# Elementwise work of GpSimd moved to VectorE in an attention, MLP and mixture-of-experts kernel

## Chip, core and metric

The kernel runs on one core of a Trainium2 chip. The metric is device time in microseconds (us), median of several executions; lower is better. Times of single instructions come from one execution taken with the hardware profiler.

## What is computed

Linear attention, a dense MLP and a top-1 mixture of experts run one after the other, all in float32 (4608 tokens, 512 features; the MLP has 2048 hidden features, each of 8 experts 1024):

```python
kv  = einsum('bhsd,bhse->bhde', k, v);  o = einsum('bhsd,bhde->bhse', q, kv)
x   = o / sqrt(mean(o*o) + 1e-6) * g_norm                     # as 4608 x 512
h   = x @ w_in;  x = (h * clip(h + 3, 0, 6) / 6) @ w_out      # float64 weights
do  = x @ w_skip > 0;  e = argmax(x[do] @ w_gate);  p = softmax(...)[e]
out = x;  out[do] += p * (relu(x[do] @ w1[e]) @ w2[e])
```

## The kernel before

**Three products for one.** A float32 product is made of three products of a faster format. Each operand is split into a high part (a copy by ScalarE, rounded) and a low part (operand minus high part, a two-input subtraction from SBUF). The products are high x high, high x low and low x high. So every weight, query, token column and gate value costs one ScalarE copy and one subtraction.

**The dense part.** Attention works on 16 units of 288 tokens, each in 4 pairs of heads; the MLP on 18 chunks of 256 tokens, each in 16 steps `f` of 128 hidden features. A step is `G1` (12 matmuls of 256 columns into `h`, L665), the gate `G1e`, and `G2` (6 matmuls of 512 columns into `y`, L656). The gate is four operations in a row: ScalarE `relu` (L701), VectorE `mul` (L706), ScalarE `high` (L710), and `low` (L716). The first two chunks run side by side while the MLP's weights are still being made.

**The weights of the MLP** are float64 and arrive as raw bits in 32 pieces: 16 for `w_in`, 16 for `w_out`, alternately. `convert` makes one piece in seven steps: `c1` to `c4` on VectorE (L600, L604, L607, L611), `c5` (L615), `high` on ScalarE (L618), `low` (L621). Four pieces can be under way: there are four staging slots in `SG` (a slot is loaded anew once `c5` has read it), and four buffers of the pool `row`.

**The routing.** After a chunk, nine scalar products on each of its two token tiles (`dot`, L768), the choice of an expert, a slot number, and a scatter of (token, gate) into a table by an indirect DMA of GpSimd (L857).

**The order.** Nothing is issued in the order of the Python text while the plan is open: `Plan.order` is a list scheduler. Each operation has an engine, a nominal cost, the operations it depends on, tokens of buffers, and a priority: the longest way from it to the end, plus a bias of its kind from the table `BIAS`. Whenever an engine is free in this calculation, the ready operation with the highest priority is taken. The outcome is a fixed order on each engine; on the chip each engine runs its own list strictly in order. Operations marked `"VP"` may go to VectorE or to GpSimd, whichever is free first, at 2.05 times the cost on GpSimd. Marked so are the low parts of queries (`ql`, L344), squares (`A2l`, L405), token columns (`Xl`, L515, and L460), the gate (`g`, step 4, L716), the last conversion pass `c5` (L615), the low parts of the MLP's weights (L621) and of the first experts' weights (`wlo`, L565).

**The experts.** Eight experts follow, by slots of up to 512 tokens in straight program order. While one computes, the weights of the next are split, 16 pieces an expert, by `w_split`: ScalarE makes the high part, and the low part goes to GpSimd for every third piece (`sp`: `n % 16 % 3 == 2`; two of 16 with at most 128 tokens), to VectorE for the others (L565). GpSimd also gathers the token rows (L900) and scatters the results (L932) by indirect DMA.

Of the kernel before, what the change touches and what calls it, by code (L numbers as in the profile page):

```python
# [16 lines left out]
NE, EFF = 8, 1024  # L17
# [34 lines left out]
class Plan:  # L52
    """Emission order of the dense part: a list schedule of operations on the engines.

    An operation has a name, an engine ("PE", "A", "V", "P", "S" for DMA queues, "VP" for either
    of two, "-" for none), a nominal cost, the names it depends on, and tokens of buffers that it
    takes and gives back. Those on the longest way to the end go first, but for a bias of their kind."""
# [31 lines left out]
    def order(self):  # L89
# [24 lines left out]
        wait = {e: [] for e in self.ENGINES}  # operations whose predecessors have started  # L114
        giving, t, dma_free, n_left = [], 0.0, 0.0, len(ops)

        def add_wait(i):
            eng = ops[i][1]
            for e in ("V", "P") if eng == "VP" else (eng,):
                r = 0.0  # L120
                for j in preds[i]:
                    fin, ej = done[j]
                    r = max(r, fin + (0.0 if e == "-" or ej == e == "PE" else self.SAME if ej == e else self.LAT))
                wait[e].append((-prio[i], i, r))
# [4 lines left out]
        while n_left:  # L129
            keep, nxt = [], []  # L130
            for g in giving:
                if g[0] <= t + 1e-9:
                    self.free[g[1]] += 1
                else:
                    keep.append(g)
                    nxt.append(g[0])
            giving = keep
            for e in self.ENGINES:
                if busy[e] > t + 1e-9:
                    nxt.append(busy[e])  # L140
                    continue
                best = None
                for w in wait[e]:
                    if w[1] in start:
                        continue
                    if w[2] > t + 1e-9:
                        nxt.append(w[2])
                    elif best is None or w < best:
                        take = ops[w[1]][5]
                        if all(self.free[k] >= take.count(k) for k in take):  # L150
                            best = w
                if best is None:
                    continue
                i = best[1]
                _, eng, cost, _, _, take, give, dma, _ = ops[i]
                wait[e] = [w for w in wait[e] if w[1] not in start and w[1] != i]
                for k in take:
                    self.free[k] -= 1
                start[i] = t
                fin = busy[e] = t + (cost * 2.05 if eng == "VP" and e == "P" else cost)  # L160
                if e == "S":
                    dma_free = max(fin + self.DMA_ISSUE, dma_free) + dma
                    fin = dma_free + self.DMA_LAT
                else:
                    fin += dma
                done[i] = (fin, e)
                giving += [(fin + self.LAT * (e != "-"), k) for k in give]
                nxt += [busy[e], fin, t + 1e-6 if e == "-" else fin]
                n_left -= 1
                for j in succs[i]:  # L170
                    left[j] -= 1
                    if not left[j]:
                        add_wait(j)
                        nxt.append(t + 1e-6)
            if n_left:
                nxt = [x for x in nxt if x > t + 1e-9]
                assert nxt, [o[0] for i, o in enumerate(ops) if i not in start and not left[i]]
                t = min(nxt)
# [5 lines left out]
def fused_kernel(ctx, tc, qT, kvm, kvr, gv, w_in, w_out, w9, w9t, w1, w2, cst, tokid, out):  # L184
# [24 lines left out]
    def op(name, eng, cost, fn, deps=(), take=(), give=(), dma=0.0, bonus=0.0):  # L209
        """into the plan, while there is one; emitted at once afterwards"""  # L210
        if plan[0] is not None:
            plan[0].add(name, eng, cost, fn, deps, take, give, dma, bonus)
        else:
            fn("V" if eng == "VP" else eng)

    # ---- constants: cst = [blockones 128 | identity 128 | triu 128 | iota 8 | ebase 8]
# [14 lines left out]
    # weights: 8 slots of 4 x 128 rows x 512, high and low parts; the last four hold attention  # L231
    # operands first
# [15 lines left out]
    # token columns: 3 slots of 4 x 128 features x 256 tokens, high and low parts  # L248
# [11 lines left out]
    # ================= attention =================  # L260
# [29 lines left out]
    # units 0 and 1 run before the tensor engine is busy: plain float32 products  # L290
# [44 lines left out]
    def st_q(u, p):  # L335
# [12 lines left out]
        op(("ql", u, p), "VP", 0.37, low, [("qh", u, p)], give=["q"] if u >= 3 else [])  # L348
# [8 lines left out]
    def prev(name, u, p):  # L357
        """from unit 2 on, pairs pass a stage in their order"""
        return [(name, u, p - 1) if p else (name, u - 1, 3)] if (u, p) > (2, 0) else []

    # accumulators: units 0 and 1 have banks that the dense MLP does not use yet
# [28 lines left out]
    def st_A2(u, p):  # L390
# [19 lines left out]
        if u >= 3:  # L410
            op(("A2h", u, p), "A", 0.33, high, [("A2", u, p)], take=["ss", "ss"])
            op(("A2l", u, p), "VP", 0.37, low, [("A2h", u, p)], give=["a"])
# [37 lines left out]
    def st_late():  # L450
        # chunk 3's first columns, kept until chunk 0 has left its buffer
# [11 lines left out]
        op("late l", "VP", 0.5, low, ["late h"], give=["row"])  # L463

    def st_N(u, p):
        # one Newton step on r = rsqrt(m / D + eps): r (3 - (m / D + eps) r^2) / 2
# [26 lines left out]
    def st_X(u, p):  # L493
# [7 lines left out]
        for c, off, done, n in parts:  # L501
# [21 lines left out]
            else:  # L523
                op(("Xh", u, p, c), "A", ca, high, [("N2", u, p)] + [("G1", c - 3, 15)] * (c >= 3))
                op(("Xl", u, p, c), "VP", cv, low, [("Xh", u, p, c)])
# [3 lines left out]
    # ================= weights =================  # L529
# [16 lines left out]
    # float32 weights of the experts, half a slot at a time through three buffers  # L546
# [20 lines left out]
    def w_split(g, j, pool=False):  # L567
        w_high(g, j)
        w_low(g, j, "P" if pool else "V")
        if j == 1:  # L570
            w_load(g + 3)

    # float64 weights arrive as raw bits: (low word, high word) of each element
# [3 lines left out]
    def convert(n, key, i):  # L577
        """float64 piece n to high and low parts.
        float32 bits = sign and top exponent bit | the rest of the exponent, mantissa"""
# [29 lines left out]
        def c4(_):  # L609
            # float32(low word) * 2^-52 * 2^exponent, added to the high word's value  # L610
# [31 lines left out]
        op(N("sg"), "VP", 0.6, c5, [N(4)])  # L642
        op(N("h"), "A", 0.52, high, [N("sg")] + war)
        op(N("l"), "VP", 0.6, low, [N("h")], give=["row"])
        op(("w", key, i), "-", 0.0, lambda _: None, [N("l")], bonus=SLACK.get("w", 0))

    # ================= dense MLP =================
    g_t, y_t = {}, {}

    def mm3(prods, first=True, last=True):  # L650
        """prods: (psum, (stationary high, low), (moving high, low)); the low moving or
        stationary part that is made last comes last"""
# [40 lines left out]
    def G1e(c, f):  # L693
# [29 lines left out]
        op(("g", c, f, 4), "VP", 0.34, low, [("g", c, f, 3)], give=[tk])  # L723
# [36 lines left out]
    # ================= routing =================  # L760
# [47 lines left out]
    def route(i):  # L808
        """routing of token tile i as operations"""
# [53 lines left out]
    def rt_bump():  # L863
        # expert 0's next free slot is at least 256 from here on
# [15 lines left out]
    # ================= experts =================  # L880
    # sets of (token columns high and low, token rows, table entries)
# [3 lines left out]
    def scatter_free(group, inst):  # L885
        """rows of one scatter are never those of another"""
# [5 lines left out]
    def ix_load(ix, row0, nt):  # L892
        """table entries of nt * 128 slots from row0 (an expression)"""
        nc.sync.dma_start(ix[:, 0:nt, :], tab[bass.ds(row0, nt * 128), :].rearrange("(t p) c -> p t c", p=128))

    def f_load(st, nt, ntok=NTOK):
        """token rows; a slot without a token keeps the row it had"""
# [40 lines left out]
    def VN(e, st, nt, side=(), late=False):  # L938
        """nt * 128 tokens, nt from 2 to 4;
        late: the side work of a step comes after its second product"""  # L940
# [27 lines left out]
        def g2(f):  # L968
# [7 lines left out]
            else:  # L976
                # tile by tile, so that the first ones leave early
# [18 lines left out]
    def V128(e, st, side=(), first=()):  # L996
        """up to 128 tokens"""
# [5 lines left out]
        def g1(hf, half):  # L1003
# [6 lines left out]
            if half == 1:  # L1010
                h = st[2][1 + hf]  # not in use with one tile of tokens
# [31 lines left out]
    # ================= emission =================  # L1043
# [14 lines left out]
    # ---- attention, and the dense MLP: chunks 0 and 1 side by side while the weights arrive  # L1058
# [58 lines left out]
    # the first experts' weights take the places of the dense ones  # L1117
# [11 lines left out]
    for g in range(11):  # L1129
# [3 lines left out]
        if g < 8:  # L1133
            for i in range(2):
                user = ("G1" if n % 2 == 0 else "G2", C, 3 + 4 * (n // 2))
                op(("wh", g, i), "A", 0.52, lambda _, g=g, i=i: w_high(g, i), [("wl", g), user])
                op(("wlo", g, i), "VP", 0.6, lambda e, g=g, i=i: w_low(g, i, e), [("wh", g, i)], bonus=10)
# [5 lines left out]
    # ---- block (0, 0), with the routing of the last chunk beside it  # L1143
    la, lb = 2 * NCH - 2, 2 * NCH - 1

    def sp(n0, n1):
        """splits of pieces, 16 to an expert"""
        return [lambda n=n: w_split(n // 2, n % 2, n % 16 % 3 == 2) for n in range(n0, min(n1, 16 * NE))]
# [20 lines left out]
    # ---- the rest of expert 0, then the other experts  # L1169
    for k in range(NE):  # L1170
# [18 lines left out]
        def tail():  # L1189
            """slots from 512 on"""  # L1190
# [26 lines left out]
        with c1.Else():  # L1217
            with tc.If(n_k > off + 128) as c2:
                VN(k, cur, 2, side(10, (5, 6, 7, 8), 2))
            with c2.Else():  # L1220
                sd = [[] for _ in range(11)]
                for q, (m0, m1) in V128_SPLITS.items():
                    m0, m1 = (max(n1 - 16 + m, n0) for m in (m0, m1))
                    sd[q] += [lambda n=n: w_split(n // 2, n % 2, n % 16 in (9, 13)) for n in range(m0, min(m1, 16 * NE))]
# [42 lines left out]
```

## Time and profile before

| | |
|---|---|
| median of 3 runs | 1375.92 us (1373.79 to 1377.61) |
| span of the profiled execution | 1371.7 us, 4.2 us less than the median |
| TensorE busy | 1254.1 us (91%), 7449 matmuls |
| VectorE busy | 895.2 us (65%), 2412 instructions |
| ScalarE busy | 600.7 us (44%), 1520 instructions |
| GpSimd busy | 405.5 us (30%), 424 instructions |

The span runs from the first to the last instruction. Busy is the time in which an engine had an instruction under way; a matmul's end is modelled, so a TensorE that is busy all the time need not run at its peak. The shares are averages over stages that differ a lot; the stages are seen in the rows below.

### The profile page before, as it was taken

Reading aid. Unit: us, or ns where it says so; the run is one execution under the profiler, and the core shown is the slowest. Engines: PE = TensorE matmul, PEld = TensorE weight load, DVE = VectorE, ACT = ScalarE, POOL = GpSimd, SP = SyncE. Lnnn points to the kernel's source line nnn. Section 1 sums busy time; section 2 is a strip of 40 time slices with the busy share of each in tenths; the row PEclk is TensorE's granted clock in tenths of the full one; section 3 lists DMA queues with packets and bytes.
Section 4 is the critical chain, followed back from the end, with each engine's and each line's share of the span. In section 5 each row is a group of like instructions: output and inputs, shape, how many; then the busy total and the mean of one; then the engine's idle time right before and its main releaser. Section 6 shows DMA issues by size and latency. Waiting matters only on the chain.

```text
span 1371.7 us, 21419 instructions
## 1 busy us (share of the span) xinstructions
PE 1254.1 (91%) x7449; PEld 1111.5 (81%) x7449; DVE 895.2 (65%) x2412; ACT 600.7 (44%) x1520; POOL 405.5 (30%) x424
## 2 busy tenths in 40 slices
PE   5788799999999999999999999999989867789895
PEld 4666688898889899999989999999878757768774
DVE  4999989748875757866767767775744344444531
ACT  2543364536563336545546546533533344324320
POOL 2656644314421103212212212200432333321411
PEclk9799999999999999999999999999999989999998
DMA  9333352211121111211121111001442355443500
GB/s 289 99 106 118 97 176 66 75 36 48 49 67 35 49 36 36 74 58 35 59 74 43 51 58 48 6 32 62 138 144 83 107 160 160 133 128 96 165 23 32
DMA packets 77449, 114.94 MB, mean 84 GB/s; under 512 B 16934, under 2 KB 38326, under 8 KB 77136
## 3 DMA queue, kind: packets, MB, share of 16 engines
q1 hardware_dynamic: 71184, 98.12, 23.0%
q0 software_dynamic: 6080, 14.57, 3.3%
q8 instruction: 89, 1.46, 0.5%
q14 instruction: 96, 0.79, 0.2%
HBM read 90.19 MB, written 25.79 MB: 85 GB/s over the span
## 4 chain that ended last, share of the span: by engine, by line
PE 68%; DVE 16%; issue 8%; DMA 4%; ACT 2%; POOL 1%; another core or an unknown queue 1%; SPq 0%; DVEq 0%; POOLq 0%; ACTq 0%
PE h L665 33%; PE y L656 29%; DVE junk L768 3%; DMA rows<-y_scr,idx 3%; PE kvp L300 2%; DVE wbits L604 2%; DVE SG L611 2%; DVE SG L607 2%; DVE t L706 1%; DVE wbits L600 1%; PE xp L912 1%; DMA sh<-cst 0%; DMA q<-qT 0%; PE h L656 0%
## 5 line engine op out<-in xcount | busy, mean ns | idle before, releaser
L768 DVE CUSTOM_DVE_ANT_0 junk<-ysb,w9b 128x512 bf16<-128x512 f32 x306 | 226.0, 739 | 4.9 <-ACT ysb L747 2.3
L701 ACT ACTIVATE t<-h,half 128x256 f32<-128x256 f32 x288 | 135.9, 473 | 205.8 <-PE h L665 104.1
L716 POOL TENSOR_TENSOR gl<-t,gh 128x256 fp32r<-128x256 f32 x120 | 103.3, 862 | 318.2 <-ACT gh L710 212.2
L710 ACT ACTIVATE gh<-t 128x256 fp32r<-128x256 f32 x288 | 119.5, 415 | 156.1 <-DVE t L706 104.6
L706 DVE SCALAR_TENSOR_TENSOR t<-t,h 128x256 f32<-128x256 f32 x288 | 119.5, 416 | 73.6 <-ACT t L701 71.7
L965 DVE SCALAR_TENSOR_TENSOR gl<-h,gh 128x256 fp32r<-128x256 f32 x64 | 27.1, 423 | 150.9 <-ACT gh L964 150.8
L716 DVE TENSOR_TENSOR gl<-t,gh 128x256 fp32r<-128x256 f32 x168 | 81.1, 483 | 63.4 <-PE y L656 31.9
L656 PE MATMUL y<-WH,gh 128*128 128x512 f32 x360 | 117.8, 405 | 0.0
L656 PE MATMUL y<-WH,gl 128*128 128x512 f32 x360 | 113.0, 391 | 3.6 <-DVE gl L716 3.6
L656 PE MATMUL y<-wh,gh 128*128 128x512 f32 x352 | 114.5, 404 | 1.2 <-ACT gh L710 1.1
L656 PE MATMUL y<-WL,gh 128*128 128x512 f32 x360 | 113.4, 392 | 0.0
L656 PE MATMUL y<-wl,gh 128*128 128x512 f32 x352 | 110.8, 394 | 1.7 <-DVE wl L621 1.7
L656 PE MATMUL y<-wh,gl 128*128 128x512 f32 x352 | 110.0, 391 | 0.1
L665 PE MATMUL h<-x12h,WH 128*128 128x256 f32 (+1 forms) x480 | 85.1, 301 | 24.7 <-issue 17.6
L964 ACT ACTIVATE gh<-h 128x256 fp32r<-128x256 f32 x64 | 24.5, 383 | 187.9 <-PE h L665 187.8
L665 PEld LDWEIGHTS h<-x12h,WH 128*128 128x128 f32 x480 | 75.7, 197 | 36.2 <-issue 18.6
L665 PE MATMUL h<-x12h,WL 128*128 128x256 f32 (+1 forms) x480 | 83.4, 297 | 0.0
L656 PEld LDWEIGHTS y<-WH,gl 128*128 128x128 f32 x360 | 67.4, 188 | 19.6 <-DVE gl L716 4.4
L665 PE MATMUL h<-x12l,WH 128*128 128x256 f32 (+1 forms) x480 | 82.5, 295 | 0.0
L656 PEld LDWEIGHTS y<-wl,gh 128*128 128x128 f32 x352 | 66.3, 189 | 18.1 <-DVE wl L621 2.6
L656 PEld LDWEIGHTS y<-WL,gh 128*128 128x128 f32 x360 | 67.8, 188 | 15.7
L656 PEld LDWEIGHTS y<-wh,gl 128*128 128x128 f32 x352 | 66.0, 188 | 15.6 <-DVE gl L716 0.6
(216 smaller groups left out, 2855.8 us busy)
## 6 DMA issues: line engine op xcount, KB each, us to landing
kv<-kvm SPq DMA_DIRECT2D x24, 512.0 KB, 4.1
stgh<-w SPq DMA_DIRECT2D x22, 512.0 KB, 3.7
stgl<-w SPq DMA_DIRECT2D x21, 512.0 KB, 4.0
stg<-w SPq DMA_DIRECT2D x21, 512.0 KB, 4.0
y_scr<-ysb SPq DMA_DIRECT2D x36, 256.0 KB, 2.5
final<-ysb SPq DMA_DIRECT2D x36, 256.0 KB, 2.7
SG<-w_in SPq DMA_DIRECT2D x16, 512.0 KB, 3.7
SG<-w_out SPq DMA_DIRECT2D x16, 512.0 KB, 3.5
```

The costliest lines, as they stand in the source:

```text
L300: nc.tensor.matmul(ps, t[0:n, 0, i, :], t[0:n, 1, i, :], start=(i == 0), stop=(i == 4))
L604: nc.vector.scalar_tensor_tensor(t, H, -(1 << 30), t, op0=ALU.bitwise_and, op1=ALU.bitwise_or)
L607: nc.vector.tensor_scalar(H, conv[n], -(1 << 23), None, op0=ALU.bitwise_and)
L611: nc.vector.scalar_tensor_tensor(f32(L), L.bitcast(U32), 2.0 ** -52, f32(H), op0=ALU.mult, op1=ALU.mult)
L656: nc.tensor.matmul(ps, st[a], mv[b], start=first and (a, b) == (0, 0) and all(p[0] is not ps for p in prods[:q]), stop=last and (a, b) == ...
L665: nc.tensor.matmul(ps, st[a], mv[b], start=first and (a, b) == (0, 0) and all(p[0] is not ps for p in prods[:q]), stop=last and (a, b) == ...
L701: nc.scalar.activation(t, h_t[c, f], ACTF.Relu, bias=half, scale=1.0 / 6.0)
L706: nc.vector.scalar_tensor_tensor(t, t, 1.0, h_t.pop((c, f)), op0=ALU.min, op1=ALU.mult)
L710: nc.scalar.activation(gh, g_t[c, f], ACTF.Copy)
L716: eng_of[e].tensor_tensor(gl, t, f32(gh), op=ALU.subtract)
L768: nc.vector.tensor_tensor_reduce(junk, ysb[i], W9["t"][:, j, :], 1.0, 0.0, ALU.mult, ALU.add, accum_out=lg[:, j:j + 1])
L965: nc.vector.scalar_tensor_tensor(gl, ps[:, c0:c0 + w], 0.0, f32(gh), op0=ALU.max, op1=ALU.subtract)
```

## The change

Every operation that was `"VP"` becomes `"V"`, so that VectorE alone does it. The scheduler loses its choice between two engines; its costs and biases stay as they are, and the order is worked out anew with them. In the experts `w_split` loses its `pool` argument. GpSimd keeps its indirect DMAs, two plain DMAs at the start, the load of the routing weights and its memsets. (The rest of the diff deletes comments.)

```diff
@@ class Plan, order
-            for e in ("V", "P") if eng == "VP" else (eng,):
-                ...
+            r = 0.0
+            for j in preds[i]:
+                ...
+            wait[eng].append((-prio[i], i, r))
-                fin = busy[e] = t + (cost * 2.05 if eng == "VP" and e == "P" else cost)
+                fin = busy[e] = t + cost
@@ queries, squares, token columns
-        op(("ql", u, p), "VP", 0.37, low, [("qh", u, p)], give=["q"] if u >= 3 else [])
+        op(("ql", u, p), "V", 0.37, low, [("qh", u, p)], give=["q"] if u >= 3 else [])
-            op(("A2l", u, p), "VP", 0.37, low, [("A2h", u, p)], give=["a"])
+            op(("A2l", u, p), "V", 0.37, low, [("A2h", u, p)], give=["a"])
-        op("late l", "VP", 0.5, low, ["late h"], give=["row"])
+        op("late l", "V", 0.5, low, ["late h"], give=["row"])
-                op(("Xl", u, p, c), "VP", cv, low, [("Xh", u, p, c)])
+                op(("Xl", u, p, c), "V", cv, low, [("Xh", u, p, c)])
@@ conversion of the MLP's weights
-        op(N("sg"), "VP", 0.6, c5, [N(4)])
+        op(N("sg"), "V", 0.6, c5, [N(4)])
-        op(N("l"), "VP", 0.6, low, [N("h")], give=["row"])
+        op(N("l"), "V", 0.6, low, [N("h")], give=["row"])
@@ gate
-        op(("g", c, f, 4), "VP", 0.34, low, [("g", c, f, 3)], give=[tk])
+        op(("g", c, f, 4), "V", 0.34, low, [("g", c, f, 3)], give=[tk])
@@ weights of the experts
-    def w_split(g, j, pool=False):
+    def w_split(g, j):
         w_high(g, j)
-        w_low(g, j, "P" if pool else "V")
+        w_low(g, j, "V")
-                op(("wlo", g, i), "VP", 0.6, lambda e, g=g, i=i: w_low(g, i, e), [("wh", g, i)], bonus=10)
+                op(("wlo", g, i), "V", 0.6, lambda e, g=g, i=i: w_low(g, i, e), [("wh", g, i)], bonus=10)
-        return [lambda n=n: w_split(n // 2, n % 2, n % 16 % 3 == 2) for n in range(n0, min(n1, 16 * NE))]
+        return [lambda n=n: w_split(n // 2, n % 2) for n in range(n0, min(n1, 16 * NE))]
```

## Rows read from the trace of the kernel before

**Rows 1.** The page's first line: the span.
```profile
span 1371.7 us, 21419 instructions
```
**Rows 2.** Busy time by stretch: PE, PEld, DVE, ACT, POOL (instructions), granted clock, DMA.
```profile
34.00:190.00 156.00, 124.13 (x681) 105.22 (x681) 151.66 (x232) 69.48 (x172) 96.09 (x83) 0.90 0.35 106
190.00:254.00 64.00, 62.59 (x407) 55.66 (x406) 55.29 (x189) 33.52 (x95) 25.44 (x30) 1.00 0.35 117
411.00:480.00 69.00, 69.00 (x451) 62.33 (x451) 45.01 (x168) 23.57 (x59) 9.13 (x10) 1.00 0.14 42
...
1000.00:1372.00 372.00, 306.23 (x1501) 265.01 (x1499) 149.49 (x276) 116.41 (x262) 103.07 (x91) 0.92 0.36 110
```
**Rows 3.** Waits of TensorE, 0 to 206 us: total, times, longest (us).
```profile
PE h L665 <- DVE t L706: 22.1, 17, 3.5
```
**Rows 4.** Timeline from 140 us: start, duration (us), engine, line, operation, [idle before].
```profile
140.66 1.41 POOL L621 TENSOR_TENSOR wl<-wbits,wh 128x512 fp32r<-128x512 f32 x1 [0.74 <-ACT wh L618]
140.84 1.78 DVE L621 TENSOR_TENSOR wl<-wbits,wh 128x512 fp32r<-128x512 f32 x1
142.54 0.41 DVE L607 TENSOR_SCALAR SG<-wbits 128x512 int32<-128x512 int32 x1
142.88 0.41 DVE L600 TENSOR_SCALAR wbits<-SG 128x512 int32<-128x512 int32 x1
```
**Rows 5.** One line's instructions: duration ns min/median/max, first and last start (us).
```profile
L604 DVE SCALAR_TENSOR_TENSOR wbits<-SG,wbits x32: 675/686/1781, 19.9 to 176.7; 128x512 int32<-128x512 int32 x32
...
L615 DVE TENSOR_TENSOR wbits<-wbits,SG x10: 677/680/1018, 21.8 to 167.9; 128x512 f32<-128x512 f32 x10
...
L716 DVE TENSOR_TENSOR gl<-t,gh x168: 409/424/1516, 66.5 to 988.6; 128x256 fp32r<-128x256 f32 x168
```
**Rows 6.** VectorE's groups, 0 to 190 us: count, busy us, mean ns, idle before.
```profile
L604 DVE SCALAR_TENSOR_TENSOR wbits<-SG,wbits 128x512 int32<-128x512 int32 x32 | 31.6, 993 | 0.1
L611 DVE SCALAR_TENSOR_TENSOR SG<-SG 128x512 f32<-128x512 uint32 x32 | 29.4, 924 | 0.1
L607 DVE TENSOR_SCALAR SG<-wbits 128x512 int32<-128x512 int32 x32 | 25.2, 793 | 0.1
L600 DVE TENSOR_SCALAR wbits<-SG 128x512 int32<-128x512 int32 x32 | 18.6, 582 | 0.0
...
L621 DVE TENSOR_TENSOR wl<-wbits,wh 128x512 fp32r<-128x512 f32 x8 | 10.6, 1330 | 0.4 <-ACT wh L618 0.3
...
L716 DVE TENSOR_TENSOR gl<-t,gh 128x256 fp32r<-128x256 f32 x6 | 5.9, 976 | 0.0
```
**Rows 7.** GpSimd's groups in the same stretch.
```profile
L615 POOL TENSOR_TENSOR wbits<-wbits,SG 128x512 f32<-128x512 f32 x22 | 32.2, 1465 | 32.4 <-DVE SG L611 19.0 <-issue 7.4 <-PE y L656 5.9
L716 POOL TENSOR_TENSOR gl<-t,gh 128x256 fp32r<-128x256 f32 x26 | 25.6, 988 | 6.6 <-ACT gh L710 3.5 <-DVE wl L621 2.4 <-PE y L656 0.7
```
**Rows 8.** Timeline of TensorE from 405 us.
```profile
405.46 0.64 PE L665 MATMUL h<-x0h,WH 128*128 128x256 f32 x4
...
406.89 0.63 PE L656 MATMUL y<-WH,gh 128*128 128x512 f32 x2
...
408.28 0.62 PE L656 MATMUL y<-WH,gh 128*128 128x512 f32 x2
```
**Rows 9.** Two lines, as in rows 5: the copies of finished chunks, the gate.
```profile
L747 ACT ACTIVATE ysb<-y x36: 575/591/602, 193.8 to 993.8; 128x512 f32<-128x512 f32 x36
...
L706 DVE SCALAR_TENSOR_TENSOR t<-t,h x288: 402/420/424, 54.3 to 990.6; 128x256 f32<-128x256 f32 x144
```
**Rows 10.** An expert's gathers on GpSimd's timeline.
```profile
1117.43 1.48 POOL L900 DMA_INDIRECT rows<-y_scr,idx  x1 [0.30 <-issue]
1119.22 1.01 POOL L900 DMA_INDIRECT rows<-y_scr,idx  x1 [0.30 <-issue]
```
**Rows 11.** Waits of TensorE, 950 to 1372 us.
```profile
PE xp L912 <- DMA rows<-y_scr,idx: 0.9, 1, 0.9
```

More of the change, by code (lines that the diff above doesn't have):

```diff
@@ L118, in add_wait @@
             eng = ops[i][1]
-            for e in ("V", "P") if eng == "VP" else (eng,):
[L120 to L124, printed above, removed]
+            r = 0.0
+            for j in preds[i]:
+                fin, ej = done[j]
+                r = max(r, fin + (0.0 if eng == "-" or ej == eng == "PE" else self.SAME if ej == eng else self.LAT))
+            wait[eng].append((-prio[i], i, r))
         for i in range(len(ops)):
@@ L213, in op @@
         else:
-            fn("V" if eng == "VP" else eng)
+            fn(eng)
     ident = cpool.tile([128, 128], F32, name="ident")
@@ L1223, in fused_kernel @@
                     m0, m1 = (max(n1 - 16 + m, n0) for m in (m0, m1))
-                    sd[q] += [lambda n=n: w_split(n // 2, n % 2, n % 16 in (9, 13)) for n in range(m0, min(m1, 16 * NE))]
+                    sd[q] += [lambda n=n: w_split(n // 2, n % 2) for n in range(m0, min(m1, 16 * NE))]
                 if k + 1 < NE:
```

## The prediction

> **What bounds the kernel now.** I read the busy time by stretch first, because the page's shares are averages over stages with different limits. The reader is to see three stages [rows 2]. From 34 to 190 us VectorE is busy 151.7 of 156 us (97%) and GpSimd 96 us, while TensorE has gaps; this is where the MLP's weights are converted and the first two chunks run. In the dense stretch after it, 411 to 480 us for one, TensorE is busy all 69 us and VectorE 45. With the experts, from 1000 us on, VectorE is busy 149 of 372 us and no engine is full. The waits of TensorE say the same: in the first 206 us it waited 22.1 us for the gate's VectorE step, which frees the `h` banks [rows 3]. So VectorE sets the end of the first stage, TensorE's own rate the dense one. The first chunk's result is copied out at 193.8 us and the last one's at 993.8 [rows 9]; a shift of the first passes on to the end.
>
> Second, the single durations. VectorE's conversion step L604 takes 675 ns at its shortest and 1781 at its longest [rows 5], and its mean in the first stage is 993 [rows 6]. The timeline shows why: GpSimd's subtraction runs from 140.66 to 142.07 us, VectorE's of the same size starts at 140.84 and ends at 142.62, which is 0.55 us after GpSimd's end [rows 4]. VectorE did not share, it stood until GpSimd was done, for 1.1 us. A VectorE instruction that reads a PSUM tile shows nothing of the kind: L706 lies between 402 and 424 ns in all its 288 instances [rows 9].
>
> **The first stage, VectorE's work.** What is added, at the shortest durations, since GpSimd will no longer be in the way: of 32 pieces VectorE did `c5` 10 times, so 22 come to it, at 0.677 us, 14.9 us [rows 5]. Of the 32 low parts of the weights it also did 10, and 22 come to it; same size and form, 14.9 us. 26 low parts of gates at 0.409, 10.6 us [rows 5, 7]. Sum 40.4 us. Instructions that follow each other on VectorE overlap a little (142.54 + 0.41 = 142.95, but the next starts at 142.88 [rows 4]), so 70 more of them take 70 x 0.07 = 4.9 less: 35.5 us.
>
> What goes is the standing still. Means less shortest durations [rows 4 to 6]: L604 32 x (0.993 - 0.675) = 10.2; L611, same size with two inputs, 32 x (0.924 - 0.675) = 8.0; L607 32 x (0.793 - 0.41) = 12.3; L600 32 x (0.582 - 0.41) = 5.5; L621 8 x (1.330 - 0.677) = 5.2; L716 6 x (0.976 - 0.409) = 3.4. Sum 44.6 us. Net -9.1 us. I left out small groups on both sides (17 low parts of queries, squares and columns that are added, and what the attention's steps and the rest of the low parts stood still); half of GpSimd's remaining work there against their excess makes it some 5 us better, an estimate, so -15 is the other end. I take -12: the first chunk could be out at 182 us.
>
> [...]
>
> **The first stage, the order.** The cover of the moved gate work is lost in one respect: its priority. I worked the priorities out of the kernel's own costs, dependencies and biases; they are only an order, no times. The steps of the `w_in` pieces stand between 736 and 511, `c1` to `c5` of the `w_out` pieces between 405 and 184, and the low parts of the gates of the first two chunks between 109 and 68, the last of everything (their bias is -250). On GpSimd that did no harm, as it had few rivals there. On a full VectorE they are taken when nothing else is ready. Behind such a low part stand `G2`, then the buffer `t` and so the next `relu`, and by the two `h` banks the next `G1`: TensorE. It has some room. Its steps cost 1.43 us (`G1`) and 1.39 (`G2`) [rows 8], so 32 steps are 90 us, and from the first gate at 54 us [rows 9] to 182 there are 128. So TensorE may lose 38 us there for nothing. The `w_in` pieces take 16 x 3.1 us (0.68 four times and 0.41 twice, less six overlaps) = 50 us of VectorE; from 34 us alone they would end at 84, with the attention and part of the rest before them at 130 at the latest. I take 110. If the gates run at half pace until then, 28 us of TensorE's work is done, 62 remain, and nothing is lost (172); at a quarter 14 are done and it ends at 186, +4; with none it ends at 200, +18. In the gaps while a staging slot is loaded, and between the dependent steps of a piece, VectorE has nothing better to do, so some pace is sure. I take +5, ends 0 and +18.
>
> **The second chunk after it** (190 to 254 us). VectorE has 55.3 of 64 us, GpSimd 25.4 [rows 2]. Half of that on VectorE would be 12.7, more than the 8.7 that are free: +4 at most. But part of GpSimd's time is scatters, which stay, and VectorE stands still less here too. I take +1.
>
> **The dense stretch.** From 411 to 480 us GpSimd ran only 10 instructions and VectorE carried nearly all low parts, at 45 of 69 us, with TensorE busy throughout [rows 2]. That is what the changed kernel does everywhere. 0, with ends -3 and +6 for a new order.
>
> **The experts.** By the code five of 16 splits an expert move: some 35 subtractions of 0.68 us, 24 us on an engine that is busy 149 of 372 [rows 2]; they lie beside products of the same step and are wanted only by the next expert. GpSimd's gathers and scatters are moved past them and find its queue empty. I take -1, ends -4 and +3.
>
> **Sum.** -12 + 5 + 1 + 0 - 1 = -7 us on a span of 1371.7 [rows 1]: 1364.7. The median lies 4.2 us above that span, so about 1369 us.
>
> **Rivals.**
> (A) *The gates starve.* If the low parts of the gates get less than a fifth of their pace until `w_in` is done, and this is late, TensorE's 90 us come after it. At 130 us with a quarter done (19 us), 71 remain: 201 us, 7 later than now; with none, 220, or 26 later. That gives 1383 to 1402, by the middle 1390. It decides from the point where fewer than a fifth of the 32 gates are through by 110 us. For it speaks the bias, against it the idle moments of VectorE in the plan.
> (B) *No relief.* The long durations have another cause and stay. Then +35.5 of VectorE work in the full stage: about 1411. The exact fit of the ends in rows 4 speaks against it.
> (C) *VectorE becomes the bound in the dense stretch.* Its list is now one strict line with gates, scalar products and low parts; a bias table made for two engines orders it. At 1 us a chunk, 16 us: 1385. The 411 to 480 us stretch speaks against it.
> (D) *It cancels.* The order eats the relief, within 4 us of now: 1375.
> (E) *Descriptors.* While two splits ran on VectorE a gather took 1.48 us, without them 1.01 [rows 10]. With more splits on VectorE, four gathers of each of eight experts could come 0.47 us later each: 32 x 0.47 = 15 us if TensorE waited for all of it, 1384. It waited 0.9 us in all for gathered rows [rows 11]. [...]
>
> **How the numbers follow.** Forecast 0.50, A 0.20, B 0.03, C 0.05, D 0.20, E 0.02. About 0.3% (4 us) is what a measurement here can tell from no change. Faster by more: 0.50, the forecast. Within: 0.20, D. Slower: 0.30, A, B, C and E. The range: the forecast's good ends (-15, 0, 1, -3, -4: -21) give about 1355; upwards it takes in C, E and most of A, up to 1396, and leaves out B, the worst of A and what lies under 1354, under 2 in 10.
>
> **What would show it.** Right: L604, L611, L607 and L600 at 0.68 and 0.41 us with no long ones, VectorE's first stage still near 97% full, the first chunk's copy at 182 to 190 us, the last copy 800 us after it as now. Wrong by A: the first chunk's copy after 200 us, few L716 before 110. Wrong by C: TensorE waiting for L716 or L706 between 260 and 990 us. Wrong by B: long VectorE durations with GpSimd idle.

## The result, and the profile after

The changed kernel takes 1393.91 us (median of 4 runs, 1391.74 to 1395.84) where the kernel before takes 1376.76 beside it: 1.0135 times as long, interval 1.0115 to 1.0154. That ratio says slower by 1.35%, the two medians themselves say 1.25% (17.2 us); the forecast was faster by 0.5%. Line numbers of the changed kernel are two below those of before for the lines named here (L604 is now L602, L716 is L714, L747 is L745).

The page of the changed kernel, span and busy time (share, instructions):

```profile
span 1393.0 us, 21133 instructions
...
PE 1258.2 (90%) x7449; PEld 1113.0 (80%) x7449; DVE 897.4 (64%) x2725; ACT 602.1 (43%) x1520; POOL 104.4 (7%) x111
```

The change did what it says: GpSimd falls from 405.5 to 104.4 us. VectorE has 313 more instructions and is busy for the same time, 897.4 us where it was 895.2. The standing still that is gone has paid for the work that came to it. And yet the span grew by 21.3 us. Of these some 4 us are a matter of which executions were profiled: the span before lies 5.1 us under the median above, the span after 0.9 us under its median.

VectorE's groups from 0 to 190 us (count, busy us, mean ns, idle before), the same view as in [rows 6]:

```profile
L602 DVE SCALAR_TENSOR_TENSOR wbits<-SG,wbits 128x512 int32<-128x512 int32 x32 | 22.0, 691 | 0.1
L609 DVE SCALAR_TENSOR_TENSOR SG<-SG 128x512 f32<-128x512 uint32 x32 | 22.0, 693 | 0.0
...
L598 DVE TENSOR_SCALAR wbits<-SG 128x512 int32<-128x512 int32 x32 | 13.7, 427 | 3.3 <-DMA SG<-w_out 3.1
L605 DVE TENSOR_SCALAR SG<-wbits 128x512 int32<-128x512 int32 x32 | 13.5, 428 | 0.1
```

993 ns became 691, 924 became 693, 793 became 428, 582 became 427. Busy time by stretch of the changed kernel (PE, PEld, DVE, ACT, POOL with instructions, granted clock with 1.00 as full speed, DMA share, GB/s), the same view as in [rows 2]:

```profile
34.00:190.00 156.00, 107.52 (x567) 90.38 (x567) 132.78 (x298) 61.81 (x145) 0.54 (x1) 0.77 0.37 111
60.00:120.00 60.00, 24.19 (x88) 18.44 (x89) 56.99 (x118) 19.80 (x43) 0.00 (x0) 0.59 0.47 140
120.00:190.00 70.00, 64.95 (x394) 57.87 (x394) 50.60 (x110) 25.08 (x54) 0.54 (x1) 0.93 0.29 95
411.00:480.00 69.00, 69.00 (x449) 62.67 (x448) 42.73 (x146) 32.37 (x85) 1.94 (x2) 1.00 0.14 42
```

The same view of the kernel before, for the second of these stretches:

```profile
60.00:120.00 60.00, 48.22 (x280) 41.31 (x279) 58.88 (x88) 26.55 (x65) 37.40 (x33) 0.94 0.39 106
```

From 60 to 120 us VectorE is as full as before, but TensorE does 88 matmuls where it did 280. Over the first stage, 34 to 190 us, VectorE has 23 us free where it had 4 [rows 2], and TensorE has lost 17 us of work. Single lines of the changed kernel (duration ns min/median/max, first and last start), the same views as in [rows 5] and [rows 9]:

```profile
L619 DVE TENSOR_TENSOR wl<-wbits,wh x16: 683/692/711, 80.3 to 168.5; 128x512 fp32r<-128x512 f32 x16
...
L714 DVE TENSOR_TENSOR gl<-t,gh x288: 411/424/449, 100.8 to 1015.4; 128x256 fp32r<-128x256 f32 x144
...
L745 ACT ACTIVATE ysb<-y x36: 578/592/605, 209.2 to 1017.4; 128x512 f32<-128x512 f32 x36
```

Two lines of the kernel before, in the same form:

```profile
L716 POOL TENSOR_TENSOR gl<-t,gh x120: 718/796/1222, 57.5 to 991.9; 128x256 fp32r<-128x256 f32 x120
...
L621 DVE TENSOR_TENSOR wl<-wbits,wh x8: 674/1360/1786, 124.8 to 184.6; 128x512 fp32r<-128x512 f32 x8
```

The low part of the last weight starts at 168.5 us; in the kernel before it was 184.6. The first chunk leaves at 209.2, where it was 193.8. So the conversion ended 16 us sooner and the chunk that needs it 15 us later. The first low part of a gate comes at 100.8 us; before, the first of them (on GpSimd) started at 57.5, and twelve of the 32 were through by 110.

**Where the 21.3 us are.** The copies of the third and fourth chunks, first before, then after (start, us):

```profile
254.63 1.08 ACT L747 ACTIVATE ysb<-y 128x512 f32<-128x512 f32 x2
300.17 1.07 ACT L747 ACTIVATE ysb<-y 128x512 f32<-128x512 f32 x2
```

```profile
262.44 0.60 ACT L745 ACTIVATE ysb<-y 128x512 f32<-128x512 f32 x1 [0.50 <-PE y L654]
...
326.35 1.07 ACT L745 ACTIVATE ysb<-y 128x512 f32<-128x512 f32 x2
```

To the first copy: 209.2 - 193.8 = +15.4. From there to the third chunk's copy: 53.2 - 60.8 = -7.6. From there to the fourth's: 63.9 - 45.5 = +18.4 (the last two together +10.8). From there to the last copy: 691.0 - 693.6 = -2.6. From the last copy to the end: 375.6 - 377.9 = -2.3. Sum +21.3.

TensorE's waits from 0 to 206 us in the changed kernel (us in total, times, longest), the same view as in [rows 3]:

```profile
PE y L654 <- DVE gl L714: 25.1, 3, 13.2
PE y L654 <- ACT WH L616: 7.3, 1, 7.3
```

Before, TensorE waited 22.1 us in 17 short pieces for the gate's product. Now it waits 25.1 us in three long ones for the gate's low part, and once 7.3 us for the high part of a weight. SyncE's loads of staging slots (start, us, count) show a second thing, here in the changed kernel:

```profile
27.03 0.33 SPq L635 DMA_DIRECT2D SG<-w_out  x1
27.45 0.39 SPq L635 DMA_DIRECT2D SG<-w_in  x1
...
35.66 20.72 SPq L635 DMA_DIRECT2D SG<-w_in  x4
...
61.35 0.39 SPq L635 DMA_DIRECT2D SG<-w_in  x1
...
67.02 0.39 SPq L635 DMA_DIRECT2D SG<-w_in  x1
...
74.14 5.70 SPq L635 DMA_DIRECT2D SG<-w_in  x2
84.42 1.54 SPq L635 DMA_DIRECT2D SG<-w_out  x2
```

and in the kernel before, the pieces of `w_out` in the same time:

```profile
38.76 0.34 SPq L637 DMA_DIRECT2D SG<-w_out  x1
...
57.55 0.34 SPq L637 DMA_DIRECT2D SG<-w_out  x1
...
77.14 2.15 SPq L637 DMA_DIRECT2D SG<-w_out  x2
```

Between 27.03 and 84.42 us the changed kernel loads not one piece of `w_out`: nine of `w_in` in a row. The kernel before loads four pieces of `w_out` in that time. `G2` multiplies with `w_out`. So two of its operands are late at once, the low part of the gate and the weight.

### The profile page after: what moved, and what is told of

Read it like the earlier page. It is cut to its first block, busy times and chain, and to the rows that moved or that the text cites. A ratio compares the mean times of both kernels' runs of the same rounds, so it can differ in the third digit from the quotient of the medians.

```text
span 1393.0 us, 21133 instructions
## 1 busy us (share of the span) xinstructions
PE 1258.2 (90%) x7449; PEld 1113.0 (80%) x7449; DVE 897.4 (64%) x2725; ACT 602.1 (43%) x1520; POOL 104.4 (7%) x111
## 4 chain that ended last, share of the span: by engine, by line
PE 69%; DMA 10%; issue 10%; DVE 8%; ACT 1%; another core or an unknown queue 1%; SPq 0%; POOL 0%; POOLq 0%; ACTq 0%; DVEq 0%
PE h L663 32%; PE y L654 30%; DMA final<-rows,idx 4%; PE kvp L298 3%; DMA rows<-y_scr,idx 3%; DMA SG<-w_out 2%; DVE wbits L613 1%; DVE SG L609 1%; DVE wbits L602 1%; DMA stgl<-w 1%; PE o L377 1%; PE o L378 1%; PE o L379 1%; DMA sh<-cst 1%
## 5 line engine op out<-in xcount | busy, mean ns | idle before, releaser
L766 DVE CUSTOM_DVE_ANT_0 junk<-ysb,w9b 128x512 bf16<-128x512 f32 x306 | 210.8, 689 | 5.8 <-ACT ysb L745 3.8
L714 DVE TENSOR_TENSOR gl<-t,gh 128x256 fp32r<-128x256 f32 x288 | 121.4, 423 | 75.3 <-PE y L654 44.5
L654 PE MATMUL y<-WH,gl 128*128 128x512 f32 x360 | 114.7, 397 | 25.1 <-DVE gl L714 25.1
L855 POOL DMA_INDIRECT tab<-pay,slot x36 | 36.4, 1011 | 803.5 <-DVE slot L850 716.2
```

The costliest lines, as they stand in the source:

```text
L654: nc.tensor.matmul(ps, st[a], mv[b], start=first and (a, b) == (0, 0) and all(p[0] is not ps for p in prods[:q]), stop=last and (a, b) == ...
L714: eng_of[e].tensor_tensor(gl, t, f32(gh), op=ALU.subtract)
L766: nc.vector.tensor_tensor_reduce(junk, ysb[i], W9["t"][:, j, :], 1.0, 0.0, ALU.mult, ALU.add, accum_out=lg[:, j:j + 1])
L855: inst = nc.gpsimd.indirect_dma_start(out=tab[:, :], out_offset=bass.IndirectOffsetOnAxis(ap=slot[:, :1], axis=0), in_=pay[:, i, :], in_of ...
```

## Experiments

Three theories of the lost start were put up. First: only the low parts of the gates starve (rival A as it was written). Second: they and the pieces of `w_out` starve together, and freeing one only brings the other out. Third: VectorE simply has too much to do in the first stage, whatever the order. Line numbers shift a little from run to run: the copies of finished chunks are L745 to L748, in tuned L827, and the gate's low part is L714 or L715.

**low_up: the gates' low parts first.** One bias of the changed kernel.

```diff
-    ("g", 2): 212, ("g", 3): -72, ("g", 4): -250, ("g", 5): -26, ("g", 6): 7, ("g", 7): -184, ("g", 8): 155,
+    ("g", 2): 212, ("g", 3): -72, ("g", 4): 200, ("g", 5): -26, ("g", 6): 7, ("g", 7): -184, ("g", 8): 155,
```

> The changed kernel with one number changed: the bias of the low parts of the gates of the first two chunks is 200 instead of -250, so that their priority (559 to 518) stands above the w_out pieces of the weights and beside the last w_in pieces. Theory 1 (the low parts of the gates starve, as the prediction's rival A said): the first chunk's copy comes before 190 us instead of 209, the whole takes about 1372 us. Theory 2 (the w_out pieces starve as well, and G2 needs them): little is gained, first copy at 203 to 213 us, 1388 to 1398 us. Theory 3 (VectorE alone has too little capacity, the order does not matter): first copy at 209, 1394 us.

Measured: 1389.87 us, 1.0096 times before (1.0063 to 1.0129). Seven low parts are through by 110 us, where the changed kernel has one, but the first copy comes at 211.7. TensorE's waits from 0 to 236 us:

```profile
PE y L654 <- ACT WH L616: 18.2, 3, 7.3
PE h L663 <- DVE t L704: 14.0, 12, 1.6
```

The wait for `gl` is gone, and a wait for the converted weight `WH` has taken its place, with twelve short ones for the gate's product `t`. The first theory falls: the gates alone, at this priority, are not it.

**out_up: `w_out` as early as `w_in`.** The pieces of `w_out` get a kind of their own, with 331 more in their bias.

```diff
+    ("co", 0): 371, ("co", 1): 349, ("co", 2): 214, ("co", 3): 191,
...
-            return ("ld" if name[2] == "ld" else "c", n // 8)
+            return ("ld" if name[2] == "ld" else "co" if n % 2 else "c", n // 8)
```

> The changed kernel with the w_out pieces of the weights raised by 331, so that each stands beside its w_in piece; the low parts of the gates stay last (bias -250). Theory 1 and 2: the gates wait until nearly all 32 pieces are made, TensorE starts later still; first chunk's copy at 220 to 240 us, 1405 to 1425 us. Theory 3 (capacity): 209 and 1394 us as in the changed kernel.

Measured: 1419.98 us, 1.0326 (1.0292 to 1.0361), the first low part of a gate at 133.7, the first copy at 234.3. TensorE's waits from 0 to 236 us:

```profile
PE y L655 <- DVE gl L715: 35.9, 2, 31.0
```

With more work ahead of them, the gates starve longer, one of them 31.0 us. Alone this too is no cure.

**both_up: both.** The two edits together, with `("g", 4)` at 400 instead of 200, so that the gates' low parts stand above the raised pieces too.

```diff
+    ("co", 0): 371, ("co", 1): 349, ("co", 2): 214, ("co", 3): 191,
...
-    ("g", 2): 212, ("g", 3): -72, ("g", 4): -250, ("g", 5): -26, ("g", 6): 7, ("g", 7): -184, ("g", 8): 155,
+    ("g", 2): 212, ("g", 3): -72, ("g", 4): 400, ("g", 5): -26, ("g", 6): 7, ("g", 7): -184, ("g", 8): 155,
...
+            return ("ld" if name[2] == "ld" else "co" if n % 2 else "c", n // 8)
```

> The changed kernel with both: w_out pieces raised by 331 and the low parts of the gates of the first two chunks at bias 400 (above all pieces). Theory 2: TensorE is fed early; first chunk's copy at 185 to 195 us, 1370 to 1382 us. Theory 1: about as much as with the gates' bias alone. Theory 3 (capacity): 209 and 1394 us.

Measured: 1374.05 us, 0.9987 (0.9972 to 1.0003). The copies of the finished chunks, and busy time by stretch:

```profile
L746 ACT ACTIVATE ysb<-y x36: 578/592/608, 187.4 to 996.2; 128x512 f32<-128x512 f32 x36
```

```profile
60.00:120.00 60.00, 34.07 (x180) 29.22 (x180) 56.63 (x128) 25.64 (x65) 0.00 (x0) 0.69 0.42 111
120.00:190.00 70.00, 70.00 (x452) 63.98 (x451) 56.48 (x126) 30.22 (x68) 0.53 (x1) 1.00 0.33 105
```

The first copy is at 187.4, 21.8 us sooner than with the change alone, by the order of the same work on the same engine. The second theory holds and the third falls. One thing more: by 110 us only five low parts are through here, fewer than in low_up with its seven, and still the chunk ends 24 us sooner than there. From 120 us on TensorE is busy all 70 us at full clock, because weights and gates are both there. How many gates are through by 110 us is therefore not what decides. Two things stay open: the gates at 400 without the raised `w_out` were not run (that this would not do is argued from low_up, where no wait for `gl` was left to cure), and both_up still stands once for 16.4 us for the gate's product `t` (L705), which now starts at 93.9 us.

**both_dot: the scalar products last.** What both_up had not given back lies behind the first copy: its fourth chunk's copy is at 305.31, 117.9 us after the first, about as long as with the change alone (117.1; before 106.3). The stretch from the third copy to the fourth, in the changed kernel and then in the kernel before:

```profile
262.00:326.00 64.00, 58.20 (x366) 51.67 (x365) 41.30 (x145) 30.49 (x80) 3.23 (x4) 0.95 0.11 33
```

```profile
254.60:300.00 45.40, 45.40 (x294) 40.98 (x294) 28.40 (x97) 17.64 (x45) 8.80 (x11) 1.00 0.08 27
```

Part of the longer time is work that has only passed from one side of the third copy to the other: 366 matmuls here where there were 294, and 331 where there were 384 in the stretch from the first copy to the third. But TensorE also stands here for 5.8 us, and before for none. The changed kernel's TensorE there (start, us, operands, [idle before]):

```profile
265.74 0.40 PE L377 MATMUL o<-qh,kh 128*128 128x288 f32 x1 [2.69 <-DVE r L480]
...
267.77 0.61 PE L419 MATMUL m<-sh,boR 128*128 128x288 f32 x1 [1.16 <-ACT sh L397]
268.91 0.61 PE L420 MATMUL m<-sl,boR 128*128 128x288 f32 x1 [0.54 <-DVE sl L403]
...
270.64 1.06 PE L663 MATMUL h<-x0h,WL 128*128 128x256 f32 x4
...
273.05 0.64 PE L663 MATMUL h<-x0h,WL 128*128 128x256 f32 x4
```

TensorE stands for attention steps of VectorE, whose priority is lower (210) than that of the scalar products of finished chunks (454 to 398 for the first eight token tiles; priorities are worked out from the kernel's costs, dependencies and biases), and then needs 1.06 us for four matmuls that take it 0.64 a little later: its granted clock was 0.52 from 269 to 273 us and 1.00 from 273 to 280. In both_up the same four took 1.05 us from 248.64 us on and 0.64 from 253.97. The edit on top of both_up:

```diff
-    ("c", 0): 40, ("c", 1): 18, ("c", 2): -117, ("c", 3): -140, ("dot", 0): 140, ("dot", 1): 61,
+    ("c", 0): 40, ("c", 1): 18, ("c", 2): -117, ("c", 3): -140, ("dot", 0): -150, ("dot", 1): 61,
```

> As the run with both biases raised, and the scalar products of the first eight token tiles lowered (bias -150 instead of 140), so that on VectorE the attention steps of unit 3 come before them. There TensorE stood 6 us at 241 to 247 us for unit 3 and then ran at half the clock until 252. Theory (this second place is a matter of order too): no such stop, the fourth chunk's copy 104 us after the second's as in the kernel before (now 113.5), total 1362 to 1368 us. Rival (VectorE is full there, so that what is brought forward pushes something else back): fourth chunk's copy 113 us after the second's as now, 1372 to 1378 us.

Measured: 1364.93 us, 0.9928 (0.9908 to 0.9948). The first and last copies, and that of the fourth chunk:

```profile
L746 ACT ACTIVATE ysb<-y x36: 581/591/608, 187.6 to 986.5; 128x512 f32<-128x512 f32 x36
```

```profile
294.92 1.07 ACT L746 ACTIVATE ysb<-y 128x512 f32<-128x512 f32 x2
```

The fourth chunk now leaves 107.3 us after the first (before 106.3, with the change alone 117.1), and the rest follows at the old length. With the biases of three kinds changed (the pieces of `w_out`, the gates' low parts, the first scalar products), the change is faster than the kernel before, at a span of 1362.3 us.

**dummy: GpSimd's work alone.** Is it GpSimd's presence that made VectorE stand? The changed kernel with 64 subtractions on GpSimd whose results nobody reads; VectorE's planned list stays the same.

```diff
+    idle = lambda _: nc.gpsimd.tensor_tensor(junk.rearrange("p (a c) -> p a c", a=4), b4, b4, op=ALU.subtract)
...
-        op(N("sg"), "V", 0.6, c5, [N(4)])
+        op(N("sg"), "V", 0.6, c5, [N(4)]); op(("idle", n), "P", 1.23, idle, [N(1), "bo"]); op(("idle2", n), "P", 1.23, idle, [N(4), "bo"])
```

> The changed kernel, with GpSimd doing 64 subtractions of 512 elements that nobody reads, two beside each piece of the weights (after c1 and after c4), written to a spare tile; VectorE's list is the same. [...] If the long durations of the kernel before had another cause (rival B): durations and time as in the changed kernel, 1394 us.

Measured: 1429.7 us, 1.0388 (1.0354 to 1.0422). GpSimd's group, VectorE's groups from 20 to 90 us, a piece of the timeline, the low parts of the weights, and the copies:

```profile
L574 POOL TENSOR_TENSOR junk<-boR 128x512 bf16<-128x512 f32 x64 | 76.8, 1200 | 15.6 <-DVE boR L1051 10.7
```

```profile
L609 DVE SCALAR_TENSOR_TENSOR SG<-SG 128x512 f32<-128x512 uint32 x5 | 7.1, 1422 | 0.0
L602 DVE SCALAR_TENSOR_TENSOR wbits<-SG,wbits 128x512 int32<-128x512 int32 x6 | 6.5, 1081 | 0.0
```

```profile
57.62 8.99 POOL L574 TENSOR_TENSOR junk<-boR 128x512 bf16<-128x512 f32 x7
...
59.13 0.51 DVE L480 SCALAR_TENSOR_TENSOR sl<-o,g_sb,sl 128x288 f32<-128x288 f32 x1
59.56 0.44 DVE L476 SCALAR_TENSOR_TENSOR sl<-m,sl 128x288 f32<-128x288 f32 x1
...
61.59 1.52 DVE L602 SCALAR_TENSOR_TENSOR wbits<-SG,wbits 128x512 int32<-128x512 int32 x1
```

```profile
L619 DVE TENSOR_TENSOR wl<-wbits,wh x16: 677/684/693, 115.7 to 201.7; 128x512 fp32r<-128x512 f32 x16
```

```profile
L745 ACT ACTIVATE ysb<-y x36: 578/592/602, 243.2 to 1053.1; 128x512 f32<-128x512 f32 x36
```

76.8 us of subtractions on the other engine move the last weight from 168.5 to 201.7 us and the first copy from 209.2 to 243.2. Steps of 691 to 693 ns take 1081 and 1422 on average while GpSimd subtracts. The two steps of this piece that read a PSUM tile (L480, L476) take 0.51 and 0.44 us in the middle of it, where their medians in the changed kernel are 0.52 and 0.45.

**experts_only: the experts' part alone.** The kernel before, with only `w_split` moved to VectorE.

```diff
-        return [lambda n=n: w_split(n // 2, n % 2, n % 16 % 3 == 2) for n in range(n0, min(n1, 16 * NE))]
+        return [lambda n=n: w_split(n // 2, n % 2) for n in range(n0, min(n1, 16 * NE))]
...
-                    sd[q] += [lambda n=n: w_split(n // 2, n % 2, n % 16 in (9, 13)) for n in range(m0, min(m1, 16 * NE))]
+                    sd[q] += [lambda n=n: w_split(n // 2, n % 2) for n in range(m0, min(m1, 16 * NE))]
```

> The kernel before with only the splits in the experts' straight program moved to VectorE; the planned dense part is the same to the last instruction. The prediction gave this part -1 us (ends -4 and +3). If the splits matter neither way: 1372 to 1377 us, no difference that can be told. If VectorE's standing still beside GpSimd's splits was on the path: the stretch from the last chunk's copy to the end falls from 378 us to 374 or less, total below 1373. If gathers are held up by VectorE (rival E): the stretch grows by 4 to 15 us.

Measured: 1374.08 us, 0.9999 (0.9984 to 1.0014). The copies:

```profile
L747 ACT ACTIVATE ysb<-y x36: 576/590/602, 194.8 to 994.4; 128x512 f32<-128x512 f32 x36
```

From the last copy to the end of the span of 1372.6 it is 378.2 us, where it was 377.9. This part of the change is worth nothing that can be told, either way. Nor does the median gather grow longer with all splits on VectorE: in the changed kernel it is 1018 ns, the longest 1539 (L898), where they were 1028 and 1480.

**before_bias: the three biases with GpSimd kept.** Are these biases simply better ones? The same edits as in both_dot, on the kernel before.

```diff
+    ("co", 0): 371, ("co", 1): 349, ("co", 2): 214, ("co", 3): 191,
+    ("c", 0): 40, ("c", 1): 18, ("c", 2): -117, ("c", 3): -140, ("dot", 0): -150, ("dot", 1): 61,
...
+    ("g", 2): 212, ("g", 3): -72, ("g", 4): 400, ("g", 5): -26, ("g", 6): 7, ("g", 7): -184, ("g", 8): 155,
```

> A control: the kernel before, with GpSimd's share of the work kept, and the three biases of the faster VectorE-only run (w_out pieces +331, low parts of the first gates 400, first scalar products -150). If those biases are simply better, this is also below 1376, at 1362 to 1370 us. If they help only where VectorE does the work alone (GpSimd had fed the gates already, and VectorE's standing still remains): not faster, 1378 to 1400 us.

Measured: 1396.07 us, 1.014 (1.0117 to 1.0164), first copy at 211.4. One group of VectorE from 0 to 190 us:

```profile
L605 DVE SCALAR_TENSOR_TENSOR wbits<-SG,wbits 128x512 int32<-128x512 int32 x32 | 31.5, 991 | 0.1
```

With two engines the same biases cost as much as the change did, and the conversion step is as long as in [rows 6], 991 ns. So an order fits one division of the work and not the other, in both directions.

**tuned: an order for one engine.** both_dot with biases chosen anew by the length of the scheduler's own plan, 23 of the table's 97 entries; some of them (the old lines are those of the changed kernel):

```diff
-    ("N", 3): -140, ("N", 4): -52, ("X", 0): -142, ("X", 1): -54, ("X", 2): -165, ("X", 3): 110, ("X", 4): 90,
-    ("g", 9): 226, ("kv", 0): 22, ("kv", 1): 17, ("kv", 2): 17, ("kv", 3): -118, ("ld", 0): -95,
...
+    ('X', 3): 330,
...
+    ('ld', 0): 393,
...
+    ('co', 0): 561,
+    ('co', 1): 447,
```

> VectorE alone, as in the run with both biases and the scalar products lowered, with the other biases of the table chosen anew for one engine (by the length of the scheduler's own plan); no operation, cost or buffer differs. Theory (the loss of the change was its order): the first stage and the dense stretch gain once more, total 1338 to 1352 us, about 2% below the kernel before. Rival (nearly all of what order can give is already given): 1358 to 1368 us.

Measured: 1347.99 us, 0.9799 (0.9779 to 0.9819). The copies:

```profile
L827 ACT ACTIVATE ysb<-y x36: 576/592/609, 169.0 to 967.9; 128x512 f32<-128x512 f32 x36
```

VectorE alone, in an order made for it, beats both kernels by 2.0% and more. No table was chosen anew for two engines, so this doesn't show that one engine is better than two, each in its best order. The first weight loads now start at 0.8 to 2.3 us instead of 13.8; how much of the gain is from these and how much from the order of the gates was not separated.

## Why the prediction was wrong

**The bound and the relief: right.** The four conversion steps stand at 691, 693, 428 and 427 ns where 0.68 and 0.41 us were worked out, and no low part of a weight took longer than 714 ns. The last weight came 16 us sooner; -12 was taken and -15 was the good end. Rival B is out, and dummy shows the cause by itself.

**The order: the step that failed.** It was put at +5, ends 0 and +18. Without it the first copy was to come at 182; it came at 209.2, so it cost 27 us. Two parts of it were wrong.
- "Some pace is sure." One of 32 low parts was through by 110 us, not a quarter and not half (twelve in the kernel before). VectorE had nothing idle to give: from 60 to 120 us it was busy 56.99 of 60 us, with other things first.
- The step asked when `w_in` would be done. It had read the priorities of all three kinds, `w_in` 736 to 511, `w_out` 405 to 184, low parts 109 to 68, but put only the last behind the first. The middle one was starved too, from 27.03 to 84.42 us, and `G2` needs it as much. low_up and out_up each raise one and stay slower than the kernel before; both_up raises both and has the first copy at 187.4, inside the 182 to 190 of the forecast.

TensorE's "room" of 38 us was also counted at full speed. Its stretch of 60 to 120 us ran at a granted clock of 0.59 where it was 0.94. And its 128 us began with the first gate at 54 us, which in the changed kernel came at 65.2.

**Rival A: the right time, half the reason.** It had 1383 to 1402, at a chance of 0.20, and 1393.91 came. It had the gates starve and not the weight. Its deciding point, a fifth of the gates by 110 us, does not decide: low_up has seven of 32 and its first copy at 211.7, both_up has five and its first copy at 187.4.

**Behind the first copy: a loss put at nothing.** +1, +4 at most, stood for 190 to 254 us, which is the stretch to the third chunk's copy; it became 7.6 us shorter. The next stretch, to the fourth copy, fell under the dense term, 0 with ends -3 and +6, read from 411 to 480 us; it became 18.4 us longer, the two together 10.8. The balance of busy time was not what failed: VectorE was busy 41.30 of 64 us there. TensorE stood again for an order, attention steps behind scalar products, and both_dot took that away.

**The dense stretch from the fourth copy on: right.** 691.0 us from the fourth copy to the last where it was 693.6; TensorE busy all 69 us and VectorE 42.73 from 411 to 480. Rival C is out.

**Experts: right in substance.** -2.3 in the profile, -1 predicted, and nothing that can be told in experts_only. TensorE's wait for gathered rows rose from 0.9 [rows 11] to 3.2 us in the changed kernel, which lies inside that; rival E is out:

```profile
PE xp L910 <- DMA rows<-y_scr,idx: 3.2, 2, 2.8
```

The one long wait of TensorE for a split, which the prediction did not name, stayed as it was: 11.4 us before (L565), 11.8 in the changed kernel (L563).

So the forecast was right for the work and wrong for the order. both_dot, the same change with the biases of three kinds, has a span of 1362.3 us; 1364.7 was worked out. By stages, against the kernel before: -6.2 us to the first copy, +1.0 to the fourth, -2.1 to the last and -2.1 from there, where -7, +1, 0 and -1 stood in the sum. That order was chosen with the result known, so this speaks for the terms of the work and not for the forecast.

## What to carry to other kernels

When work moves to an engine that is already full, busy time tells whether it fits; it says nothing of what then waits behind it. Priorities tuned for two engines can be harmless low on the idle one and starve on the full one: list, for the operation that the bounding engine needs next, every operand and its place in the new queue, not only the moved one. Elementwise work of GpSimd between SBUF tiles cost VectorE's steps of the same kind time (dummy: means of 1081 and 1422 ns where the changed kernel has 691 and 693), so here it was worth taking away, but with an order chosen anew.

## What the runs showed of the hardware

- The starved TensorE was also a slow one here. From 60 to 120 us, with 24.19 of 60 us busy, its granted clock was 0.59 on average; with 64.95 of 70 us busy after that, 0.93. From 263 to 269 us it was busy 1.61 of 6 us; from 269 to 273 us its clock was 0.52, and four matmuls of 256 columns took 1.06 us; from 273 us on it was 1.00, and they took 0.64.
- In dummy GpSimd did not touch the tiles of the conversion, and VectorE's steps there grew longer all the same: the subtractions read one constant tile, and the 0.69 us steps on other tiles took up to 1.52 us.
